# Holding back the loads of piece 12, splitting the transposes of pieces 8 to 11, and ordering the first slices of block 1 bank by bank in a retention-then-FFN kernel

## The chip, the core and the metric

The kernel runs on one core of one Trainium2 chip. The metric is the device time of one execution in microseconds; the time before is the median of three executions. Five engines run side by side, each with its own instruction stream: PE (TensorE, matrix products), DVE (VectorE), ACT (ScalarE), POOL (GpSimd, which here only issues loads) and SP (SyncE, which here issues stores and transposes by DMA). An engine takes its instructions in order; what stands behind a waiting instruction waits too.

## What is computed

Retention (attention with a decaying mask and no softmax) over 8 batches, 8 heads, 576 positions and 64 dimensions, and then a two-layer network with a hard swish over all 4608 tokens:

```python
scores = scale * np.matmul(q, k.transpose(0, 1, 3, 2))
Dmat = np.where(rel >= 0, gamma[:, None, None] ** rel[None, :, :], 0.0)
attn = np.matmul(scores * Dmat[None], v)
x = attn.transpose(0, 2, 1, 3).reshape(B * S, H * D)        # 4608 x 512
h = x @ w_in                                                # 512 -> 2048
out = (h * np.clip(h + 3.0, 0.0, 6.0) / 6.0) @ w_out        # 2048 -> 512
```

## The kernel before

**Pieces.** The retention part is cut into pieces of 128 positions with all heads. Each batch has four "main" pieces (512 positions), and the last 64 positions of two batches together make one "rest" piece. Pieces 0 to 3 are batch 0, 4 to 7 batch 1, 8 to 11 batch 2, 12 the first rest, 13 to 16 batch 3 and so on. A piece needs its K (`kn`), its Q and V (`qv`), both transposed (`qk`), Q and V scaled by powers of the decay (`vs`), masked scores (`at`), and a state carried from piece to piece (`u` is the sum of products on PE, `ts` the scaled state on DVE, `tbd` its fp16 block-diagonal form, two copies on ACT, L394 and L395). The result `o` is copied by ACT into `xt16`, the transposed tokens (L353).

**Blocks.** The network takes 512 tokens at a time (nine blocks). GEMM1 of a block has 16 units: four matmuls into one PSUM bank `ph` (L409), then ACT's `Relu` (L416), then DVE's minimum and product into `gt` (L417), which frees the bank. There are four such banks. GEMM2 has 16 units of four matmuls (`pout`, L467); every fourth unit of a row group ends with ACT's copy (L471) and a store on SP (L453; L457 for the last block, whose rows go to two places and take two stores).

**Order.** The order is written out by hand. While block kb runs through GEMM2, the pieces of block kb+1 are computed between its units: `put(units, steps)` runs a unit, then one entry of a list `later`, then what `steps` names for that unit. `ahead(c)` prepares piece c: it loads up to piece c+4 (`load_until`) and calls `transposes_by_dma(c)`: SP transposes K, DVE scales Q and V (L306), SP transposes the scaled Q (L303). Pieces 0 to 7 are transposed on PE (`transposes_early`, `transposes`), since the first blocks can't wait for the DMA. `warm` multiplies zeros to keep PE busy at the start (L175).

**Loads.** All loads stand in POOL's stream in the order of the pieces, three to a piece (K, Q, V; six half ones for a rest piece, L91), with the weights between pieces 3 and 5 (L97, L102). The loads share eight semaphores in turn, so each one waits until the eighth load before it has landed. There are nine buffers for `kn` and `qv`, so the load of piece c also waits until piece c-9 was used.

**Block 1's first units.** Between GEMM2 of block 0 and the rest of GEMM1 of block 1, the program opens all four banks and calls `g1_columns` three times: columns 0 to 255 of all four banks, then `second_half(7)` (the result and state of piece 7), then columns 256 to 383 of all banks, then `ahead(8)`, then columns 384 to 511 of all banks, which are piece 7's tokens. As the last slice of a bank is done, ACT and DVE take that bank.

Of the kernel before, what the change touches and what calls it, by code (L numbers as in the profile page):

```python
# [13 lines left out]
ALU = mybir.AluOpType  # L14
# [3 lines left out]
def kernel(  # L18
# [66 lines left out]
    def load(c, behind_q=None):  # L85
        kn = nat.tile([P, H, D], FP16, tag="kn", bufs=9, name=f"kn_{c}")
        qv = nat.tile([P, 2, H, D], FP16, tag="qv", bufs=9, name=f"qv_{c}")
        loaded[c] = {"kn": kn, "qv": qv, "q16": qv[:, 0]}
        for dst, src in ((kn, k), (qv[:, 0], q), (qv[:, 1], v)):
            for p0, b, s0, n in pieces[c][3]:  # L90
                nc.gpsimd.dma_start(dst[p0:p0 + n],  # L91
                                    src[b, :, s0:s0 + n, :].rearrange("h s d -> s h d"))
            if src is q and behind_q is not None:
                behind_q()

# [18 lines left out]
    first = const.tile([P, 1], FP32)  # L114
# [17 lines left out]
    for p in range(NPAIR):  # L132
# [17 lines left out]
                            in1=gq[:, :, None].to_broadcast([P, H, P]), op=ALU.mult)  # L150
# [6 lines left out]
    gqv = const.tile([P, 2, H, D], FP16)  # L157
# [3 lines left out]
    tbd = []  # L161
# [8 lines left out]
    def warm(n, cols):  # L170

        w = psum.tile([P, MBLK], FP32, tag="ph", bufs=4, name=f"warm_{warmed[0]}")
        warmed[0] += 1
        for _ in range(n):
            nc.tensor.matmul(w[:, 0:cols], zeros[:, 0:P], zeros[:, 0:cols],  # L175
                             start=True, stop=True)
# [13 lines left out]
    st = {}  # L190
    later = []
# [14 lines left out]
    def transposes_early(c, alone=True):  # L206
        kn, q16 = loaded[c]["kn"], loaded[c]["q16"]
        qk = work.tile([P, 2, NPAIR, P], FP16, tag="qk", bufs=6, name=f"qk_{c}")
        st[c]["qk"] = qk
        pk = psum.tile([P, NPAIR, P], FP16, tag="ph", bufs=4, name=f"trk_{c}")  # L210
        for p in range(NPAIR):
            nc.tensor.transpose(pk[:, p, :], kn[:, 2 * p:2 * p + 2, :], ident16)
        nc.scalar.copy(qk[:, 1], pk)
        if c == 0:
            warm(6, MBLK)
        elif alone:
            warm(8, P)
        pq = psum.tile([P, NPAIR, P], FP32, tag="ph", bufs=4, name=f"trq_{c}")
        for p in range(NPAIR):
            for h2 in range(2):  # L220
                r = slice(h2 * HALF, h2 * HALF + HALF)
                nc.tensor.matmul(pq[r, p, :], q16[:, 2 * p + h2, :], dq[:, 2 * p + h2, :],
                                 start=(p == 0), stop=(p == NPAIR - 1), skip_group_check=True)
        nc.scalar.copy(qk[:, 0], pq)  # L224
        if c == 0:
            warm(8, P)

    def scores_last(c):

# [63 lines left out]
                nc.tensor.transpose(ps[:, i, p, :], src[:, 2 * p:2 * p + 2, :], ident16)  # L293
        nc.vector.tensor_copy(qk, ps)

    def transposes_by_dma(c):
        qv, kn = loaded[c]["qv"], loaded[c]["kn"]
        qk = work.tile([P, 2, NPAIR, P], FP16, tag="qk", bufs=6, name=f"qk_{c}")
        vs = work.tile([P, 2, H, D], FP16, tag="vs", bufs=6, name=f"vs_{c}")
        st[c] = {"qk": qk, "vs": vs[:, 1]}  # L300

        def transpose(which, src):
            nc.sync.dma_start_transpose(qk[:, which], src.rearrange("s h d -> s (h d)"))  # L303

        transpose(1, kn)
        nc.vector.tensor_tensor(out=vs, in0=qv, in1=gqv, op=ALU.mult)  # L306
        transpose(0, vs[:, 0])

    def scores(c):
        run_later(9)  # L310
# [58 lines left out]
                                     stop=(j == len(cs) - 1 and p == NPAIR - 1),  # L369
                                     skip_group_check=True)  # L370

    def update_state(c):
        kind, b, i, _ = pieces[c]
        if kind == "rest":
            return
        u = st[c]["u"]
        scale = gc_b[1 if i == PER - 1 and b % 2 else 0]
        ts = work.tile([P, NPAIR, D], FP16, tag="ts", bufs=2, name=f"ts_{c}")
        if i == 0:
            nc.vector.tensor_tensor(out=ts, in0=u, in1=scale, op=ALU.mult)  # L380
        else:
            ta = work.tile([P, NPAIR, D], FP32, tag="ta", bufs=2, name=f"ta_{c}")
            nc.vector.tensor_tensor(out=ta, in0=u, in1=st[c - 1]["ts"], op=ALU.add)  # L383
            nc.vector.tensor_tensor(out=ts, in0=ta, in1=scale, op=ALU.mult)  # L384
        st[c]["ts"] = ts
        old = state_of.get(b)
        new = free_tbd.pop(0)
        state_of[b] = new
        if old is not None and st[c].get("o") is not None:
            free_tbd.append(old)  # L390
        elif old is not None:
            st[c]["before"] = old
            st[c]["last_reader"] = True
        nc.scalar.copy(tbd[new][0:HALF, :, 0:D], ts[0:HALF])  # L394
        nc.scalar.copy(tbd[new][HALF:P, :, D:2 * D], ts[HALF:P])  # L395

    def finish(c):
        intra(c)
# [13 lines left out]
    def g1_act(kb, ph, fc):  # L412
        if kb not in gts:
            gts[kb] = work.tile([P, NFC, MBLK], FP16, tag="gt16", bufs=2, name=f"gt16_{kb}")
        u = work.tile([P, MBLK], FP32, tag="moeu", bufs=3, name=f"u_{kb}_{fc}")
        nc.scalar.activation(u, ph, ACTF.Relu, bias=cb[:, 0:1], scale=1.0 / 6.0)  # L416
        nc.vector.scalar_tensor_tensor(out=gts[kb][:, fc, :], in0=u, scalar=1.0,  # L417
                                       in1=ph, op0=ALU.min, op1=ALU.mult)
# [6 lines left out]
        g1_mm(kb, ph, fc, range(NCC))  # L425
        g1_act(kb, ph, fc)

    def g1_columns(kb, banks, cols):

        t0 = kb * MBLK  # L430
        for fc, ph in enumerate(banks):
            for dmc in range(NCC):
                nc.tensor.matmul(ph[:, cols], win16[:, dmc, P * fc:P * fc + P],
                                 xt16[:, dmc, t0 + cols.start:t0 + cols.stop],
                                 start=(cols.start == 0 and dmc == 0),
                                 stop=(cols.stop == MBLK and dmc == NCC - 1),
                                 skip_group_check=True)
                if dmc == NCC - 1 and cols.stop == MBLK:
                    g1_act(kb, ph, fc)

    def g1_first(kb):

# [7 lines left out]
    def store(kb, mc, cols, src):  # L450
        if kb < B:
            r0 = kb * S + P * mc
            nc.sync.dma_start(out[r0:r0 + P, cols], src)  # L453
        else:
            for i in range(2):
                r0 = (2 * mc + i) * S + MAIN
                nc.sync.dma_start(out[r0:r0 + HALF, cols], src[i * HALF:i * HALF + HALF])  # L457

    pouts = {}

# [35 lines left out]
    load(4)  # L496
    for i in range(4):
        load_wout(4 * i, 4 * i + 4)
    for c in (5, 6, 7):
# [35 lines left out]
    def second_half(c):  # L535
        inter(c)
        finish(c)

    def ahead(c):
        if c < NP:  # L540
            load_until(c + 4)
            transposes_by_dma(c)

    def scores_second(c):

# [50 lines left out]
    def gemm1(kb, steps):  # L596

        units = {0: [lambda: g1_first(kb)]}.get(kb, [])
        done = {0: 2, 1: 4}.get(kb, 0)
        put(units + [unit1(kb, f) for f in range(done, NFC)], steps)  # L600

    gemm1(0, {12: [(scale, 4)]})
# [1 line left out]
    put([unit2(0, mc, part) for mc, part in order],  # L606
        {0: [(transposes, 4)], 2: [(scores, 4)], 4: [(second_half, 4)],
         8: [(make_mask_rest,)], 10: [(early, 5)], 11: [(scores, 5)], 12: [(early, 6)],
         13: [(second_half, 5), (scores, 6)], 14: [(early, 7)],
         15: [(second_half, 6), (scores, 7)]})  # L610
    run_later(9)

    banks = [g1_bank(1, fc) for fc in range(4)]
    g1_columns(1, banks, slice(0, 2 * P))
    second_half(7)
    g1_columns(1, banks, slice(2 * P, 3 * P))
    ahead(8)
    g1_columns(1, banks, slice(3 * P, MBLK))
    gts.pop(0)


    gemm1(1, {2: [(ahead, 9)], 5: [(ahead, 10)], 8: [(ahead, 11)]})
    AT = {1: (-1, 7), 4: (-1, 7, 12), 5: (-1, 3, 7, 11)}
    for kb in range(1, NMB - 1):
        mine, next_ = of_block(kb + 1), of_block(kb + 2)
        pairs = [mine[i:i + 2] for i in range(0, len(mine), 2)]
        steps = {}
        for j, ended, begun in zip(AT[len(mine)], [[]] + pairs, pairs + [[]]):
            steps.setdefault(j, []).append((step, ended, begun))
        for c in mine[4:]:  # L630
            steps.setdefault(2, []).append((ahead, c))
        for c, j in zip(next_[:4], (12, 13, 14, 15)):
            steps.setdefault(j, []).append((ahead, c))
        put([unit2(kb, mc, part) for mc in range(MBLK // P) for part in range(4)], steps)
        gts.pop(kb)
        gemm1(kb + 1, {})
# [34 lines left out]
```

## Time and profile before

| what | value |
|---|---|
| median of 3 executions | 310.43 us (310.31 to 310.57) |
| the profiled execution | 311.39 us, of which the span 309.6 us |
| PE busy | 299.5 us (97%) |
| DVE, ACT, POOL busy | 185.8, 173.6, 108.0 us |
| loads (q0, POOL's queue) | 18.36 MB, packets 82.9% of 16 engines' span |
| stores and transposes (q1, SP's queue) | 16.79 MB, packets 27.6% |
| one load of 128 KB, issue to landing | median 6.2 to 6.5 us |
| one transpose, issue to landing | median 4.1 us, 2.4 to 8.8 |
| granted TensorE clock | 1.00 in every slice |

The profiled execution is one run with the hardware profiler on; its time is 1.8 us more than its span. In the timelines below a line gives the start, the length, the engine, the line of the kernel, the operation, its operands and sizes, and in brackets the idle time of the engine before it and what ended that. In the list of waits the numbers are microseconds in total, times, and the longest. Stretches in which an engine with slack is idle cost nothing.

### The profile page before, as it was taken

What the parts mean: (1) busy time and instruction counts of PE and PEld (TensorE: products, weight loads), DVE (VectorE), ACT (ScalarE), POOL (GpSimd) and SP (SyncE); (2) the same over time, 40 slices, a digit from 0 to 9 for tenths busy, and PEclk for the clock granted to TensorE, in tenths of its full rate; (3) what the DMA queues carried; (4) which work ended last, traced back from release to release, by engine and by line L of the source; (5) the groups of instructions that cost most, each with busy time, mean ns of one, the idle gap of its engine ahead of it and who ended that gap; (6) DMA issues with size and microseconds to landing.
All of it is one profiled execution on the core that took longest, in us unless ns stands there. A gap on an engine that the chain in (4) does not pass through costs nothing.

```text
span 309.6 us, 5856 instructions
## 1 busy us (share of the span) xinstructions
PE 299.5 (97%) x2286; PEld 152.6 (49%) x2286; DVE 185.8 (60%) x310; ACT 173.6 (56%) x298; POOL 108.0 (35%) x135
## 2 busy tenths in 40 slices
PE   8889999899999999999999999999999999999994
PEld 3644446544544554445544644455445544444443
DVE  4758715796737882885478737856688357207600
ACT  4657356773457554854574737644765467227611
POOL 8974378696735390045353720130000000000000
PEclk9999999999999999999999999999999999999999
DMA  9999999999999999539998996094423230010033
GB/s 65 145 197 190 204 156 211 168 140 156 191 174 170 114 171 163 118 24 154 146 166 74 140 184 138 17 123 69 104 51 53 83 55 0 34 70 34 1 70 68
DMA packets 153164, 35.52 MB, mean 115 GB/s; under 512 B 143792, under 2 KB 148656, under 8 KB 153136
## 3 DMA queue, kind: packets, MB, share of 16 engines
q0 software_dynamic: 117264, 18.36, 82.9%
q1 hardware_dynamic: 35872, 16.79, 27.6%
q8 instruction: 18, 0.29, 0.4%
q14 instruction: 10, 0.08, 0.1%
HBM read 36.70 MB, written 9.44 MB: 149 GB/s over the span
## 4 chain that ended last, share of the span: by engine, by line
PE 76%; DMA 16%; POOL 6%; issue 1%; DVE 0%; ACT 0%; POOLq 0%
PE pout L467 35%; PE ph L409 31%; DMA wout<-in_moe_w_out_dram 5%; POOL qv L91 4%; DMA win<-in_moe_w_in_dram 3%; DMA qv<-in_v_dram 3%; PE o L349 3%; DMA kn<-in_k_dram 3%; DMA qk<-vs 2%; POOL kn L91 2%; PE o L338 2%; PE sc L316 2%; PE u L367 1%; PE pout L480 1%; PE sc L552 1%
## 5 line engine op out<-in xcount | busy, mean ns | idle before, releaser
L417 DVE SCALAR_TENSOR_TENSOR gt<-u,ph 128x512 f16<-128x512 f32 x144 | 98.1, 687 | 69.0 <-ACT u L416 68.3
L467 PE MATMUL pout<-wout,gt 128*128 128x512 f16 x560 | 126.6, 380 | 0.0
L409 PE MATMUL ph<-xt,win 128*128 128x512 f16 x560 | 122.3, 379 | 1.4 <-DVE gt L417 1.4
L416 ACT ACTIVATE u<-ph,cb 128x512 f32<-128x512 f32 x144 | 98.5, 687 | 25.9 <-PE ph L409 25.4
L409 PEld LDWEIGHTS <-win 128*128 128x128 f16 x560 | 54.7, 98 | 67.3 <-issue 1.6
L467 PEld LDWEIGHTS <-gt 128*128 128x128 f16 x560 | 52.3, 98 | 60.8
L91 POOL DMA_DIRECT2D kn<-in_k_dram x40 | 34.4, 861 | 80.9 <-PE u L367 59.2
L471 ACT COPY osb<-pout 128x512 f32<-128x512 f32 x35 | 20.5, 585 | 48.1 <-PE pout L467 47.8
L91 POOL DMA_DIRECT2D qv<-in_q_dram x40 | 34.2, 858 | 7.4 <-DMA wout<-in_moe_w_out_dram 3.0
L320 DVE TENSOR_TENSOR at<-sc,mask_wide 128x1024 f16<-128x1024 f32 x19 | 23.2, 1223 | 22.4 <-PE sc L316 22.4
L91 POOL DMA_DIRECT2D qv<-in_v_dram x40 | 34.6, 868 | 3.2 <-DMA wout<-in_moe_w_out_dram 1.7
L394 ACT COPY tbd<-ts 64x256 f16<-64x256 f16 x28 | 11.3, 405 | 34.1 <-DVE ts L384 17.2
L353 ACT CAST xt<-o 128x512 f16<-128x512 f32 x35 | 19.3, 588 | 10.9 <-PE o L349 10.7
L306 DVE TENSOR_TENSOR vs<-qv,gqv 128x1024 f16<-128x1024 f16 x28 | 17.9, 684 | 0.0
L560 DVE TENSOR_TENSOR at<-sc,mask_wide 128x512 f16<-128x512 f32 x24 | 15.4, 681 | 0.0
L349 PE MATMUL o<-at,vs 128*64 128x128 f16 x280 | 12.2, 223 | 0.0
L395 ACT COPY tbd<-ts 64x256 f16<-64x256 f16 x28 | 11.2, 401 | 0.4
L383 DVE TENSOR_TENSOR ta<-u,ts 128x256 f32<-128x256 f32 x21 | 8.7, 416 | 3.6 <-PE u L367 3.6
L316 PE MATMUL sc<-qk 64*128 64x128 f16 x184 | 9.1, 218 | 1.2 <-ACT qk L224 1.1
L338 PEld LDWEIGHTS <-tbd 128*128 128x128 f16 x124 | 7.9, 98 | 4.5
L384 DVE TENSOR_TENSOR ts<-ta,gc 128x256 f16<-128x256 f32 x21 | 8.9, 425 | 1.7
L349 PEld LDWEIGHTS <-vs 128*64 128x64 f16 x280 | 8.6, 109 | 2.6 <-issue 0.4
(73 smaller groups left out, 120.1 us busy)
## 6 DMA issues: line engine op xcount, KB each, us to landing
out_dram<-osb SPq DMA_DIRECT2D x32, 256.0 KB, 3.5
kn<-in_k_dram POOLq DMA_DIRECT2D x32, 128.0 KB, 6.2
qv<-in_q_dram POOLq DMA_DIRECT2D x32, 128.0 KB, 6.3
qv<-in_v_dram POOLq DMA_DIRECT2D x32, 128.0 KB, 6.5
wout<-in_moe_w_out_dram POOLq DMA_DIRECT2D x4, 512.0 KB, 15.2
win<-in_moe_w_in_dram POOLq DMA_DIRECT2D x3, 512.0 KB, 10.1
out_dram<-osb SPq DMA_DIRECT2D x6, 128.0 KB, 2.3
win<-in_moe_w_in_dram POOLq DMA_DIRECT2D x2, 256.0 KB, 6.2
```

The lines of the kernel that those rows point to most:

```text
L91: nc.gpsimd.dma_start(dst[p0:p0 + n], src[b, :, s0:s0 + n, :].rearrange("h s d -> s h d"))
L306: nc.vector.tensor_tensor(out=vs, in0=qv, in1=gqv, op=ALU.mult)
L316: nc.tensor.matmul(sc[:, h2, p, :], qk[r, 1, p, :], qk[r, 0, p, :], start=True, stop=True)
L320: later.append(lambda: nc.vector.tensor_tensor(out=at.rearrange("t a b s -> t (a b) s"), in0=sc.rearrange("t a b s -> t (a b) s"), in1=mas ...
L349: nc.tensor.matmul(o[r, p, :], vs[:, 2 * p + h2, :], at[:, h2, p, :], start=(st[c]["first"] and p == 0), stop=(p == NPAIR - 1), skip_group ...
L353: nc.scalar.copy(xt16[:, :, g0:g0 + P], o)
L409: nc.tensor.matmul(ph, win16[:, dmc, P * fc:P * fc + P], xt16[:, dmc, t0:t0 + MBLK], start=(dmc == 0), stop=(dmc == NCC - 1))
L416: nc.scalar.activation(u, ph, ACTF.Relu, bias=cb[:, 0:1], scale=1.0 / 6.0)
L417: nc.vector.scalar_tensor_tensor(out=gts[kb][:, fc, :], in0=u, scalar=1.0, in1=ph, op0=ALU.min, op1=ALU.mult)
L467: nc.tensor.matmul(pout, gt[:, fc, P * mc:P * mc + P], wout16[:, fc, :], start=(fc == 0), stop=(fc == NFC - 1))
L471: nc.scalar.copy(osb, pout)
L560: nc.vector.tensor_tensor(out=at[:, h2], in0=banks[h2], in1=mask[:, None, :].to_broadcast([P, NPAIR, P]), op=ALU.mult)
```

## The change

Six edits:

1. `warm(8, P)` becomes `warm(2, MBLK)`: two matmuls of 512 columns for eight of 128, at four places.
2. `transposes_by_dma` is split in `transpose_k` and `transpose_q` (which also scales). K of piece 8 is transposed inside GEMM2 of block 0; Q of 8 ahead of piece 7's result; K and Q of 9 to 11 at units 0, 1, 5 and 9 of block 1's GEMM1. The loads of pieces 8 to 11 are issued from an earlier place in the program; POOL's order stays the same.
3. `ahead_last(11)`: the first load of piece 12 waits for DVE's scaling of piece 11.
4. `g1_columns` takes one bank at a time, and the last two slices go in an order in which bank 0 is complete after three groups of four matmuls. Piece 7's two state copies on ACT are put behind the fifth unit's activation.
5. In the last block the second store of each pair goes to ACT's queue.
6. The fifth piece of a block is prepared after unit 0 in place of unit 2. The instruction order of no engine changes by this.

```diff
@@ load
-                nc.gpsimd.dma_start(dst[p0:p0 + n],
-                                    src[b, :, s0:s0 + n, :].rearrange("h s d -> s h d"))
+                loaded[c]["dma"].append(nc.gpsimd.dma_start(
+                    dst[p0:p0 + n], src[b, :, s0:s0 + n, :].rearrange("h s d -> s h d")))
@@ transposes_early
         elif alone:
-            warm(8, P)
+            warm(2, MBLK)
...
         if c == 0:
-            warm(8, P)
+            warm(2, MBLK)
@@
-    def transposes_by_dma(c):
-        qv, kn = loaded[c]["qv"], loaded[c]["kn"]
+    def transpose_k(c):
         qk = work.tile([P, 2, NPAIR, P], FP16, tag="qk", bufs=6, name=f"qk_{c}")
+        st[c] = {"qk": qk}
+        nc.sync.dma_start_transpose(qk[:, 1], loaded[c]["kn"].rearrange("s h d -> s (h d)"))
+
+    def transpose_q(c):
         vs = work.tile([P, 2, H, D], FP16, tag="vs", bufs=6, name=f"vs_{c}")
-        st[c] = {"qk": qk, "vs": vs[:, 1]}
...
+        st[c]["vs"] = vs[:, 1]
+        scaled = nc.vector.tensor_tensor(out=vs, in0=loaded[c]["qv"], in1=gqv, op=ALU.mult)
+        nc.sync.dma_start_transpose(st[c]["qk"][:, 0], vs[:, 0].rearrange("s h d -> s (h d)"))
+        return scaled
@@ update_state(c, copies_later=False)
-        nc.scalar.copy(tbd[new][0:HALF, :, 0:D], ts[0:HALF])
-        nc.scalar.copy(tbd[new][HALF:P, :, D:2 * D], ts[HALF:P])
+        def copies():
+            nc.scalar.copy(tbd[new][0:HALF, :, 0:D], ts[0:HALF])
+            nc.scalar.copy(tbd[new][HALF:P, :, D:2 * D], ts[HALF:P])
+        if copies_later:
+            later.append(copies)
+        else:
+            copies()
@@ store
-                nc.sync.dma_start(out[r0:r0 + HALF, cols], src[i * HALF:i * HALF + HALF])
+                queue = nc.scalar if i else nc.sync
+                queue.dma_start(out[r0:r0 + HALF, cols], src[i * HALF:i * HALF + HALF])
@@
+    def ahead_last(c):
+        scaled = transpose_q(c)
+        load_until(c + 4)
+        tc.add_manual_dep(
+            loaded[c + 1]["dma"][0].ins, scaled.ins.name,
+            mybir.DependencyInfo(mybir.DependencyClass.Sync, mybir.DependencyReason.DATA),
+            reason="transposes of block 2 first")
@@ the main order
+    load_until(11)
...
-         13: [(second_half, 5), (scores, 6)], 14: [(early, 7)],
+         13: [(second_half, 5), (scores, 6)], 14: [(early, 7), (transpose_k, 8)],
...
-    g1_columns(1, banks, slice(0, 2 * P))
-    second_half(7)
-    g1_columns(1, banks, slice(2 * P, 3 * P))
-    ahead(8)
-    g1_columns(1, banks, slice(3 * P, MBLK))
+    for fc in range(4):
+        g1_columns(1, fc, banks[fc], slice(0, 2 * P))
+    transpose_q(8)
+    inter(7)
+    intra(7)
+    update_mm([7])
+    update_state(7, copies_later=True)
+    third, fourth = slice(2 * P, 3 * P), slice(3 * P, MBLK)
+    for fc, cols in ((0, third), (1, third), (0, fourth), (2, third), (1, fourth), (3, third),
+                     (2, fourth), (3, fourth)):
+        g1_columns(1, fc, banks[fc], cols)
...
-    gemm1(1, {2: [(ahead, 9)], 5: [(ahead, 10)], 8: [(ahead, 11)]})
+    gemm1(1, {0: [(transpose_k, 9)], 1: [(transpose_q, 9), (transpose_k, 10)],
+              5: [(transpose_q, 10), (transpose_k, 11)], 9: [(ahead_last, 11)]})
...
-            steps.setdefault(2, []).append((ahead, c))
+            steps.setdefault(0, []).append((ahead, c))
```

More of the change, by code (lines that the diff above doesn't have):

```diff
@@ L87, in load @@
         qv = nat.tile([P, 2, H, D], FP16, tag="qv", bufs=9, name=f"qv_{c}")
-        loaded[c] = {"kn": kn, "qv": qv, "q16": qv[:, 0]}
+        loaded[c] = {"kn": kn, "qv": qv, "q16": qv[:, 0], "dma": []}
         for dst, src in ((kn, k), (qv[:, 0], q), (qv[:, 1], v)):
             for p0, b, s0, n in pieces[c][3]:
-                nc.gpsimd.dma_start(dst[p0:p0 + n],
-                                    src[b, :, s0:s0 + n, :].rearrange("h s d -> s h d"))
+                loaded[c]["dma"].append(nc.gpsimd.dma_start(
+                    dst[p0:p0 + n], src[b, :, s0:s0 + n, :].rearrange("h s d -> s h d")))
             if src is q and behind_q is not None:
@@ L294, in transposes @@
         nc.vector.tensor_copy(qk, ps)
-    def transposes_by_dma(c):
-        qv, kn = loaded[c]["qv"], loaded[c]["kn"]
+    def transpose_k(c):
         qk = work.tile([P, 2, NPAIR, P], FP16, tag="qk", bufs=6, name=f"qk_{c}")
+        st[c] = {"qk": qk}
+        nc.sync.dma_start_transpose(qk[:, 1], loaded[c]["kn"].rearrange("s h d -> s (h d)"))
+    def transpose_q(c):
         vs = work.tile([P, 2, H, D], FP16, tag="vs", bufs=6, name=f"vs_{c}")
-        st[c] = {"qk": qk, "vs": vs[:, 1]}
[L302 to L307, printed above, removed]
+        st[c]["vs"] = vs[:, 1]
+        scaled = nc.vector.tensor_tensor(out=vs, in0=loaded[c]["qv"], in1=gqv, op=ALU.mult)
+        nc.sync.dma_start_transpose(st[c]["qk"][:, 0], vs[:, 0].rearrange("s h d -> s (h d)"))
+        return scaled
     def scores(c):
@@ L370, in update_mm, with update_state @@
                                      skip_group_check=True)
-    def update_state(c):
+    def update_state(c, copies_later=False):
         kind, b, i, _ = pieces[c]
@@ L426, in g1, with g1_columns @@
         g1_act(kb, ph, fc)
-    def g1_columns(kb, banks, cols):
+    def g1_columns(kb, fc, ph, cols):
         t0 = kb * MBLK
[L431 to L439, printed above, removed]
+        for dmc in range(NCC):
+            nc.tensor.matmul(ph[:, cols], win16[:, dmc, P * fc:P * fc + P],
+                             xt16[:, dmc, t0 + cols.start:t0 + cols.stop],
+                             start=(cols.start == 0 and dmc == 0),
+                             stop=(cols.stop == MBLK and dmc == NCC - 1),
+                             skip_group_check=True)
+        if cols.stop == MBLK:
+            g1_act(kb, ph, fc)
     def g1_first(kb):
@@ L498 @@
         load_wout(4 * i, 4 * i + 4)
-    for c in (5, 6, 7):
+    for c in range(5, 8):
         load(c)
@@ L541, in ahead @@
             load_until(c + 4)
-            transposes_by_dma(c)
+            transpose_k(c)
+            transpose_q(c)
+    def ahead_last(c):
[5 more added lines that the diff above has]
+            reason="transposes of block 2 first")
     def scores_second(c):
```

## The prediction

> **What bounds the kernel now.** The page says PE is busy for 299.5 of 309.6 us, so I looked first for where it is not. Three views were read in this order: the chain that ended last (from 71 us on it is PE without a break until the last ACT copy at 305.34), the list of PE's waits, and the timelines of single engines around those waits. PE's waits, in whole (us in total, times, longest):
>
> ```profile
> PE ph L409 <- DVE gt L417: 1.4, 1, 1.4
> PE warm L175 <- DVE cb L112: 1.3, 1, 1.3
> PE sc L316 <- ACT qk L224: 1.1, 2, 0.8
> PE trq L222 <- DMA qv<-in_q_dram: 0.9, 1, 0.9
> PE sc L552 <- DMA qk<-vs: 0.6, 1, 0.6
> PE o L258 <- DVE at L240: 0.3, 1, 0.3
> ```
>
> So at most these 5.6 us and the tail after 305.3 can be won; any larger change must be a loss. The PE timeline places them (start, length, then the idle time in brackets):
>
> ```profile
> 14.97 0.61 PE L175 MATMUL warm<-zeros 128*128 128x128 f16 x8
> 16.44 0.41 PE L222 MATMUL trq<-dq,qv 128*64 128x128 f16 x8 [0.86 <-DMA qv<-in_q_dram]
> ...
> 56.07 1.96 PE L433 MATMUL ph<-xt,win 128*128 128x128 f16 x32
> 59.47 10.52 PE L409 MATMUL ph<-xt,win 128*128 128x512 f16 x48 [1.44 <-DVE gt L417]
> 69.92 0.40 PE L316 MATMUL sc<-qk 64*128 64x128 f16 x8
> 70.96 0.40 PE L552 MATMUL sc<-qk 64*128 64x128 f16 x8 [0.64 <-DMA qk<-vs]
> ```
>
> The change works on the third (fewer zeros before 19 us), on the 1.44 and on the 0.64, and on the tail.
>
> **Fewer zeros: 0.** Eight matmuls of 128 columns hold PE for 0.54 us (9.69 to 10.23 around piece 1); two of 512 columns hold it for 0.44 (0.219 each, L409: 13.99 us for 64). That is 0.1 us at each of four places, and all four lie before the wait at 16.44. Query load 3 was issued at 10.53 and landed 5.9 us later, at 16.43: PE waits for it whatever it does before. Without that cover it would be worth 0.3 to 0.4 us. On the cost side: the first nine zeros took 4.02 us, 0.446 each, against 0.219 later, so PE does start at half speed, while the granted clock reads 1.00 throughout. [...]
>
> **Bank by bank, copies later, piece 8 scaled first: -0.78.** Now ACT and DVE go like this:
>
> ```profile
> 56.05 0.58 ACT L353 CAST xt<-o 128x512 f16<-128x512 f32 x1 [0.94 <-PE o L349]
> 57.17 0.40 ACT L394 COPY tbd<-ts 64x256 f16<-64x256 f16 x1 [0.53 <-DVE ts L384]
> 57.59 0.40 ACT L395 COPY tbd<-ts 64x256 f16<-64x256 f16 x1
> 58.01 3.21 ACT L416 ACTIVATE u<-ph,cb 128x512 f32<-128x512 f32 x5
> ```
>
> ```profile
> 54.18 1.22 DVE L320 TENSOR_TENSOR at<-sc,mask_wide 128x1024 f16<-128x1024 f32 x1
> 56.18 0.42 DVE L383 TENSOR_TENSOR ta<-u,ts 128x256 f32<-128x256 f32 x1 [0.78 <-PE u L367]
> 56.71 0.43 DVE L384 TENSOR_TENSOR ts<-ta,gc 128x256 f16<-128x256 f32 x1
> 57.05 0.68 DVE L306 TENSOR_TENSOR vs<-qv,gqv 128x1024 f16<-128x1024 f16 x1
> 58.73 3.21 DVE L417 SCALAR_TENSOR_TENSOR gt<-u,ph 128x512 f16<-128x512 f32 x5 [1.00 <-ACT u L416]
> ```
>
> PE's 32 short matmuls are eight groups of four at 0.245 us. Bank 0 ends with the fifth group, at 57.30, but ACT first does two state copies and starts on bank 0 only at 58.01. With the change the last slice of bank 0 is the third group. It needs piece 7's tokens (L353 ends at 56.63), so it runs from 56.68 to 56.93. ACT starts 0.2 us after a bank's end (59.47 + 2 x 0.863 = 61.20, next activation at 61.40): 57.13, with the copies out of the way. DVE follows 0.72 us after ACT (58.01, 58.73), at 57.85, and PE 0.74 us after that (58.73, 59.47): **58.59 instead of 59.47, -0.88**. PE's own groups end at 58.15 (the wait for L353 costs 0.12, inside the remaining idleness of 0.44). Piece 8's scaling, moved ahead of L383 on DVE, fits the gap of 0.78 us: V of piece 8 landed at 52.53 (chain), DVE is free at 55.40 and needs 0.68, to 56.08.
>
> What is late next: the two copies (0.84) now stand on ACT behind the fifth activation, at 60.33, so activations 5 to 7 are late, and piece 9's scaling (now one activation pair earlier on DVE) stands between gt 5 and gt 6. Stepping ACT by 0.64 and DVE by 0.64 back to back, gt 6 starts at 63.13, and PE's seventh 512-column unit, due at 58.59 + 6 x 0.863 = 63.77, would start at 63.87: +0.10. All other units have slack. Bounds of this step: 0 if the queues refill behind each other, -1.32 if no idleness is left.
>
> **K and Q of pieces 8-11 apart, loads of 12 on held back: -0.64.** On PE this touches one wait, for piece 9's Q transpose: issued on SP at 64.30 after its scaling, landed at 70.83, 6.5 us; all eight transposes issued from 53.67 to 69.70 took 6.5 to 8.8. Now the scaling runs after gt 5, 62.5 to 63.2, and the issue is at 63.2. PE is there at 58.69 + 12 x 0.863 + 0.33 = 69.38. So a landing within 6.2 us costs nothing. The nearest rows for a transpose with few loads beside it are those issued between 95 and 125 us (2.4 to 7.4, median 3.3); the last load ahead of it, V of piece 11, lands at 62.1 (issued 53.92, 8.2). I take 4: landing 67.2, the wait of 0.64 goes whole. [...]
>
> K of piece 8 passes the store of block 0's last rows on SP. It waits for its load (issued 42.61, about 8 us), so SP issues it near 50.6 for 1.3 us, and the store is not ready before 53.2 (L471 at 52.61 + 0.58). Behind each Q transpose on SP stands the next K transpose; 11 is issued near 69.6, due at 77.2 on PE.
>
> The added wait stands on POOL. Behind it are all loads from piece 12 on, nothing else:
>
> ```profile
> 54.88 1.40 POOL L91 DMA_DIRECT2D kn<-in_k_dram  x2
> ...
> 61.61 0.88 POOL L91 DMA_DIRECT2D kn<-in_k_dram  x1 [1.08 <-PE ph L409]
> ...
> 79.51 0.88 POOL L91 DMA_DIRECT2D kn<-in_k_dram  x1 [1.33 <-PE sc L316]
> ```
>
> Piece 12 starts at 54.88 now; then it waits for piece 11's scaling, after gt 13, done near 69.55: 14.7 us later. Six halves of 0.68 and nine loads of 0.87 follow; V of piece 15 is issued at 80.6. Loads in the quiet beginning landed 3.6 to 5.9 us after issue, those of 79.5 to 84 us 7.4 to 8.2; between them I take 6: 86.6. DVE scales piece 15 directly ahead of block 2's first gt, which must end at 90.45 so that PE's fifth unit of block 2 (88.47 - 1.42 + 4 x 0.863 = 90.50) does not wait: scaling may start at 89.1. It hides, with 2.5 us to spare. Later loads catch up: POOL idles 59 us in waits for freed buffers (L91 on PE u L367). The piece-16 and later fifth transposes move two steps ahead in the code, but on no engine does the order of instructions change: 0.
>
> **Second half stores on ACT: -0.5.** At the end SP issues two 64 KB stores one after the other:
>
> ```profile
> 302.45 4.38 SPq L457 DMA_DIRECT2D out_dram<-osb  x6
> ```
>
> Ten such issues take 466/562/588 ns (min/median/max); the last starts at 306.2 and lands about 2 us later, which ends the span. With the other half on ACT both start near 305.7. ACT's own issue is in no row: at SP's 0.56 it saves 0.56; at POOL's 0.88, 0.24; at SP's transpose issue of 1.2 nothing. I take 0.5, close to the nearest row, a store on SP. The earlier stores on ACT stand before copies that come 1.16 us or more of idleness later, so delay none.
>
> **Sum.** -0.88 + 0.10 - 0.64 - 0.5 = -1.92. The profiled execution took 311.39 us (span 309.6 and 1.8 around it), so 309.5; it lies 0.96 above the median of 310.43, and on that **308.5**.
>
> **Rivals.** *The transpose stays slow*: SP issues piece 9's Q at 63.2, and at 7.8 us (the row of the first Q transpose) it lands at 71.0, where it lands now; PE's gain at 59 us is eaten by that wait and only the tail is left: 310.43 + 0.04 - 0.5 = 310.0. For it: all eight rows; against: they all had loads beside them. *The held loads come too late* (slower): each load waits for the landing of the eighth before it, so with a landing time L V of 15 is issued at 73.7 + L, if later than 80.6. From L = 7.7 on it lands after 89.1 and PE waits in block 2; from L = 8.7 on that eats the 1.92. L was 10 between 69 and 73 us: issue 83.7, landing 93.7, PE at 95.1 instead of 90.5, net +2.7: 313.1. For it: that row, and 7.5 at 80 us; against: then eight transposes and the loads' own queue were under way, here one transpose. *More than forecast*: no wait left at 59 us and 0.56 at the tail: 310.43 - 1.32 - 0.64 - 0.56 = 307.9.
>
> **Chances.** Forecast (308.0 to 309.4) 0.70; slow transpose 0.14 (0.08 of it still faster, 0.06 about equal); late loads 0.11; more than forecast 0.05. About 0.2% (0.6 us) is what a measurement of this kernel can tell from no change. Faster 0.83, same 0.06, slower 0.11. The range 307.7 to 310.0 leaves out the late loads and little else.
>
> **What would show it.** Right: PE's wait on gt near 58.6 us at 0.4 to 0.5 in place of 1.44, no wait on L552's successor near 69.4, no new PE wait near 90, the loads of piece 12 from about 69.5, the span's end 0.5 us nearer to the last copy. Wrong: a PE wait for gt in block 2 behind piece 15's scaling, a Q transpose of piece 9 over 6.2 us, or ACT's copies showing as waits of PE between 60 and 65 us.

## The result and the profile after

The changed kernel takes **312.82 us** (median of 11 executions, 311.26 to 316.27) against 310.43 for the kernel before (310.02 to 312.27, 11 executions): slower, by a ratio of 1.0074 with an interval of 1.0044 to 1.0103. The forecast was 308.5. The ratio leaves out one execution, that of 316.27, whose granted clock was 0.988.

The profiled execution took 312.04 us, its span 310.0 (before 309.6), the clock 1.00 throughout. PE's waits in the changed kernel, in whole (total us, times, longest):

```profile
PE u L269 <- DVE vs L203: 1.5, 1, 1.5
PE sc L315 <- DMA qk<-vs: 1.4, 1, 1.4
PE warm L175 <- DVE cb L112: 1.3, 1, 1.3
PE sc L315 <- ACT qk L224: 0.4, 2, 0.3
PE ph L415 <- DVE gt L423: 0.4, 1, 0.4
PE trq L222 <- DMA qv<-in_q_dram: 0.4, 1, 0.4
```

PE's timeline of the changed kernel places them (start, length, idle time before in brackets):

```profile
18.88 0.40 PE L269 MATMUL u<-vs,kn 128*128 128x128 f16 x4 [1.46 <-DVE vs L203]
...
59.49 10.52 PE L415 MATMUL ph<-xt,win 128*128 128x512 f16 x48 [0.44 <-DVE gt L423]
69.94 0.40 PE L315 MATMUL sc<-qk 64*128 64x128 f16 x8
70.18 0.39 PE L568 MATMUL sc<-qk 64*128 64x128 f16 x8
...
112.91 0.40 PE L315 MATMUL sc<-qk 64*128 64x128 f16 x8 [1.36 <-DMA qk<-vs]
```

Of the two waits that the change aimed at, 1.44 has become 0.44 and 0.64 is gone: the scores at 69.94 and 70.18 follow each other. Two others stand in their place: 1.46 at the start, for V of piece 3, and **1.36 at 112.91**, where no wait was before. The first has a like in the kernel before, 0.86 at 16.44 for Q of piece 3, which is 0.40 now. The second is for the transposed Q of piece 16, the fifth piece in block 2's GEMM2. Here are SP's issues of that transpose, of the changed kernel and then of the one before:

```profile
106.32 1.20 SPq L305 DMA_TRANSPOSE qk<-vs  x1
```

```profile
107.02 1.19 SPq L303 DMA_TRANSPOSE qk<-vs  x1
```

Issued 0.7 us earlier than before, it lands after 6.5 us in place of 3.3. PE wants it 5.2 us after the issue in both kernels (112.91 - 1.36 - 106.32). At its issue eight loads are under way (issued and not landed) in the changed kernel, two in the kernel before. The DMA view of the stretch from 106 to 112 us shows what moved beside it: first the loads' queue of the changed kernel, then that of the kernel before (packets, MB, packet time as a share of 16 engines' span; the times of packets that overlap add up, so it can pass 100%).

```profile
q0 software_dynamic: 5351, 0.67, 240.2%
```

```profile
q0 software_dynamic: 3714, 0.47, 124.4%
```

POOL's timeline tells where these loads come from. The changed kernel:

```profile
54.90 0.89 POOL L91 DMA_DIRECT2D qv<-in_v_dram  x1
70.86 1.38 POOL L91 DMA_DIRECT2D kn<-in_k_dram  x2 [15.07 <-PE u L366]
...
81.82 1.02 POOL L91 DMA_DIRECT2D qv<-in_v_dram  x1
...
103.14 0.87 POOL L91 DMA_DIRECT2D qv<-in_v_dram  x1 [1.35 <-DMA kn<-in_k_dram]
105.69 0.69 POOL L91 DMA_DIRECT2D kn<-in_k_dram  x1 [1.68 <-DMA qv<-in_q_dram]
```

And the kernel before around the same time:

```profile
87.41 0.88 POOL L91 DMA_DIRECT2D qv<-in_v_dram  x1
94.03 1.36 POOL L91 DMA_DIRECT2D kn<-in_k_dram  x2 [5.74 <-DMA qk<-kn]
...
103.40 0.89 POOL L91 DMA_DIRECT2D kn<-in_k_dram  x1 [5.28 <-PE u L367]
```

The wait of 15.07 us is the hold; the bracket names PE, but DVE's scaling of piece 11 ended at 70.33, half a microsecond before the load starts. Before, POOL pauses at 88 and 98 us for a free buffer, and the DMA engines catch up (the load issued at 87.41 lands after 10.6 us, that at 94.03 after 5.5). After, POOL's idle time at 103 and 105 us ends on landings of earlier loads, each time 0.3 us behind that of the eighth load before: nothing waits for a buffer, the queue itself is behind. Its loads issued from 88.6 to 96 us land after 12 to 16 us; those of 94 to 98 us in the kernel before, after 5.5 to 7. The first load of piece 21 starts at 105.69, at 94.03 before: of the 15 us that the loads were held, 11.7 have not been made up when piece 16 needs a quick transpose.

Milestones that answer to the prediction's steps, from PE's timelines of before and after: start of block 0's GEMM1 to the start of block 1's long GEMM1 run 39.92 and 39.07 (-0.85); from there to the start of GEMM2's first 32 matmuls 12.20 and 11.49 (-0.71); start of the last ACT copy to the end of the span 4.25 and 3.93 (-0.32). The start of GEMM1 is 0.87 later, the new wait costs 1.4. Together that is about +0.4, the difference of the two spans.

The medians differ by 2.39, not by 0.4. The profiled execution of before lies 0.96 above its median, that of the changed kernel 0.78 below its own: 7 of the 11 executions of the changed kernel have a granted clock under 0.996, and the profiled one has not (more on that below). The rest, some 0.3 us, lies outside the span: an execution's time is 1.8 us more than its span in the kernel before and 2.0 to 2.1 in every kernel that holds the loads until piece 11 is scaled (after, and e1, e6, e8, e9, e13 and e14 below). No view shows what that is; it stays open.

### The profile page after: what moved, and what is told of

Same layout as the page of the kernel before. It is cut to its first block, busy times and chain, and to the rows that moved or that the text cites. A ratio compares the mean times of both kernels' runs of the same rounds, so it can differ in the third digit from the quotient of the medians.

```text
span 310.0 us, 5801 instructions
## 1 busy us (share of the span) xinstructions
PE 300.3 (97%) x2262; PEld 151.6 (49%) x2262; DVE 185.6 (60%) x310; ACT 173.3 (56%) x298; POOL 107.9 (35%) x135
## 4 chain that ended last, share of the span: by engine, by line
PE 87%; DMA 4%; POOL 3%; DVE 2%; ACT 1%; issue 1%; POOLq 0%; ACTq 0%
PE ph L415 39%; PE pout L473 37%; PE o L348 3%; DMA qv<-in_v_dram 2%; DMA qk<-vs 2%; POOL qv L91 2%; PE sc L315 2%; PE o L337 2%; POOL kn L91 1%; PE pout L486 1%; PE u L366 1%; PE ph L438 1%; ACT u L422 1%; PE sc L568 1%; DVE gt L423 0%
## 5 line engine op out<-in xcount | busy, mean ns | idle before, releaser
L91 POOL DMA_DIRECT2D qv<-in_q_dram x40 | 34.9, 875 | 7.5 <-DMA wout<-in_moe_w_out_dram 3.6
L175 PE MATMUL warm<-zeros 128*128 128x512 f16 x23 | 8.8, 525 | 1.3 <-DVE cb L112 1.3
```

Source lines behind the costliest of these rows:

```text
L91: loaded[c]["dma"].append(nc.gpsimd.dma_start(dst[p0:p0 + n], src[b, :, s0:s0 + n, :].rearrange("h s d -> s h d")))
```

## The experiments

Sixteen kernels ran in four groups, e1 to e4 and so on; each ratio is to executions of the kernel before on the same chip (medians 310.81, 310.56, 310.98, 310.68 in the four groups). My theory H: the added wait on POOL pushes the loads' backlog to piece 16's transpose. Rival Z: the fewer zeros cost the time, by a late or slow start.

**e1 to e4: one part undone.** e1 puts the old zeros back, e2 takes the added wait out, e3 does both, e4 puts only the fewer zeros into the kernel before.

```diff
e1, e3:  -            warm(2, MBLK)        +            warm(8, P)      (two calls)
e2, e3:  -        tc.add_manual_dep(loaded[c + 1]["dma"][0].ins, scaled.ins.name, ...)
e4, in the kernel before:  -  warm(8, P)   +  warm(2, MBLK)             (two calls)
```

> The changed kernel with the eight short zero matmuls put back at all four places, everything else as changed. Theory Z (fewer zeros let the granted PE clock fall in some executions, and that is what spreads the times from 311.3 to 316.3 us): all executions at a clock of 1.00, a spread under 0.8 us, and a median lower by 0.5 to 1.5 us, near 311. Theory H (the loads held back are the whole loss, through the 1.4 us that PE waits near 112 us for piece 16's Q transpose): no change against the changed kernel, 312 to 313 us, clocks as often below 1.00 as there. In both the wait near 112 us stays, as the loads are still held.

> The changed kernel without the wait of piece 12's first load on piece 11's scaling; everything else as changed, the few zeros too. Theory H: the wait for piece 16's Q transpose near 112 us goes (1.4 us), Q of piece 9 still lands in time or nearly, and the median falls by 1 to 1.5 us, to some 311.4. Theory Z: the spread and the clocks below 1.00 stay, and the median stays over 310.4.

> Both put back: old zeros, no held loads; what is left of the change is the bank order, the later copies, the early transposes and the stores on ACT. Theories Z and H together: 308.3 to 309.0 us with a narrow spread, faster than before by 1.4 to 2.1 us. Z alone: near 310; H alone: near 311 with a wide spread. If neither is the cause, it stays at 312 to 313.

> The kernel before with two zero matmuls of 512 columns in place of eight of 128, nothing else changed. Theory Z: the median rises over 311 us, executions differ by 2 us and more, and several show a granted clock under 1.00. Theory H: 310.4 us, as before, with the old narrow spread.

Measured: e1 311.57 us, 1.0031 [1.0013, 1.0050]; e2 309.43, **0.9962** [0.9944, 0.9979]; e3 309.35, 0.9963 [0.9948, 0.9978]; e4 311.25, 1.0028 [1.0005, 1.0050]. Without the added wait the change is a gain. PE's timeline of e2 at the same place has no bracket:

```profile
111.07 0.61 PE L337 MATMUL o<-qk,tbd 128*128 128x128 f16 x8
111.61 0.40 PE L315 MATMUL sc<-qk 64*128 64x128 f16 x8
```

The transpose lands after 4.6 us in e2 and 4.4 in e3. In e1 the wait is 1.73. H holds; Z alone doesn't, as e1 stays slower than before. Nor was the hold needed for piece 9: in e3 the Q transposes issued between 53 and 72 us take 4.7 to 8.0 us (after: 2.4 to 8.4, median 3.0), and PE still waits for none of them at 69 us. The hold was not without use: in two of the later profiles without it (e11 and e16) PE waits 0.27 and 0.59 us near 78 us for Q of piece 11, and in none with the full hold.

**e5 to e8: one part alone, and the dose.** e5 puts the second stores on ACT in the kernel before; e6 adds the hold alone to the kernel before; e7 holds the loads only until piece 9 is scaled (old zeros); e8 keeps the whole hold, with the old zeros, and prepares the fifth piece earlier, after unit 9 of the GEMM1 ahead.

```diff
e5  +  queue = nc.scalar if i else nc.sync
    +  queue.dma_start(out[r0:r0 + HALF, cols], src[i * HALF:i * HALF + HALF])
e6  +  load_until(15); tc.add_manual_dep(loaded[12]["dma"][0].ins, scaled.ins.name, ...)   (piece 11)
e7  -  5: [..., (transpose_k, 11)], 9: [(ahead_last, 11)]
    +  1: [(transpose_q_then_load, 9), ...], ... 9: [(transpose_q, 11)]
e8  -  for c in mine[4:]: steps.setdefault(0, []).append((ahead, c))
    -  gemm1(kb + 1, {})
    +  gemm1(kb + 1, {9: [(ahead, c) for c in next_[4:]]})
```

> The kernel before with the second store of each pair of the last block on ACT's queue, nothing else changed. By the profiles of the changed kernel the time from the last ACT copy's start to the end of the span is 3.9 us with ACT's queue and 4.3 to 4.8 without, so 0.3 to 0.8 us faster than before (forecast in the prediction: 0.5). If the store on ACT gives nothing, the same as before.

> The kernel before with the held loads alone (the first load of piece 12 waits for the scaling of piece 11); zeros, bank order, transposes and stores as before. Theory H: piece 16's Q transpose again takes over 6 us and PE waits 1 to 2 us for it near 113 us, in part of the executions followed by some 3.4 us at half the granted clock (1.7 us more); the wait of 0.64 us near 71 us may go. Net 0.5 to 2.5 us slower than before. Rival (the held loads only hurt together with the rest of the change, since PE reaches that place 0.7 us sooner there): no wait near 113 us and no loss.

> The changed kernel with the old zeros, and the loads of piece 12 held only until piece 9 is scaled (about 62.5 us in place of 69.6). Theory H, graded: the loads are 7 us late instead of 15, so the backlog is gone by 106 us; piece 16's Q transpose lands in under 5 us, no wait of PE near 111 us, 308.6 to 309.6 us, as without any hold. Rival: any hold costs; the wait stays at about 1 us or more.

> The changed kernel with the old zeros and the full hold, but the fifth piece of a block (16, 25 and so on) scaled and transposed within GEMM1 of the block before (after its tenth unit) and not in GEMM2. If the loss is that one late transpose, it is then issued near 99 us, lands by 107 and PE does not wait near 111 us: 308.6 to 309.6 us with the hold still in. Rival: the held loads cost elsewhere too (other transposes, contention): over 310.4 us.

Measured: e5 310.37, 0.9987 [0.9971, 1.0003], too near 1 to decide on time alone; its profile shows 3.93 us from the last copy to the end, 4.25 before. e6 311.30, **1.0039** [1.0010, 1.0068]: the hold alone makes the old kernel slower. PE's timeline of e6:

```profile
113.53 0.61 PE L317 MATMUL sc<-qk 64*128 64x128 f16 x8 [2.42 <-DMA qk<-vs]
```

The transpose lands after 7.5 us there, and the eight matmuls behind the wait last 0.61 us, not 0.40 as in the rows above (more on that below). e7 309.55, 0.9972 [0.9955, 0.9989]: under half of the hold (POOL idles 6.8 us in it, 15.1 in after), landing 4.8, no wait. e8 309.48, **0.9956** [0.9940, 0.9971], with the hold still in. SP's timeline of e8:

```profile
99.23 2.36 SPq L305 DMA_TRANSPOSE qk<-vs  x1
```

This one lands after 8.3 us, the slowest of all for piece 16's Q, and PE does not wait, as it is issued 7 us earlier. So it is the lateness of this one issue under the backlog that costs, and not the backlog elsewhere, but for the 0.3 us outside the span, which e8 has too.

**e9 to e12: the zeros, and a version that combines.** e9 is e8 with the fewer zeros; e10 is the kernel before without any zeros at the four places; e11 is e8 without the hold; e12 repeats e4.

```diff
e9   -  warm(8, P)    +  warm(2, MBLK)          (in e8, two calls)
e10  -  elif alone: warm(8, P)     -  if c == 0: warm(8, P)     (in the kernel before)
e11  -  tc.add_manual_dep(...)                  (in e8)
```

> The kernel of e8 (full hold, fifth piece prepared within GEMM1) with the few zeros of the change. If fewer zeros cost nothing: the ratio of e8, 0.994 to 0.997. If fewer zeros delay the start (in three profiles with few zeros V of piece 3 was scaled at 17.4, 18.4 and 18.5 us, in seven with the old zeros at 16.4 to 17.6): 0.5 to 1 us more, 0.996 to 0.999, and V of piece 3 again after 17.5 us.

> The kernel before without any zero matmuls at the four places that the change touches (the first nine and the six after K of piece 0 stay). If the zeros there matter through the granted clock, PE's matmuls before 20 us take their half-speed length (0.4 us for 512 columns) more often and the kernel is slower by 1 us or more. If PE is bound there by the loads of piece 3 alone: within 0.5 us of before.

> The kernel of e8 without the hold (old zeros, bank order, early transposes, stores on ACT, fifth piece prepared within GEMM1). If the hold is of no use to Q of piece 9: the same as e8 and e3, 309.0 to 309.7 us, no wait of PE near 69 and near 111 us. If the hold helps: 0.3 us or more slower than e8.

> The kernel of e4 once more (before with few zeros), since its interval of 1.0005 to 1.0050 hardly leaves 1 out. If fewer zeros cost: again 1.001 or more and V of piece 3 scaled after 17.3 us; if not: the interval takes in 1 and that scaling falls near 16.7.

Measured: e9 309.89, 0.9971 [0.9949, 0.9993]; e10 311.81, 1.0026 [1.0002, 1.0049]; e11 309.19, **0.9935** [0.9911, 0.9959], the lowest ratio here, though on six executions and with an interval that overlaps those of e8, e2 and e3; e12 310.66, 0.9994 [0.9975, 1.0014], which doesn't repeat e4's 1.0028. e10 fits neither of its expectations cleanly: some 0.8 us slower in the median, with a full clock in its profile and 5 of 12 executions under 0.996.

**e13 to e16: the four corners on one chip.** The changed kernel (e13), with the old zeros (e14), without the hold (e15), with neither (e16); the edits are those of e1 to e3.

> The changed kernel once more, side by side with its three neighbours. Its four undisturbed executions (clock 1.0) lay 1.6 us above before's median, those of the same kernel with the old zeros only 0.6 above, on another chip. Theory A (fewer zeros cost nothing while the clock stays full, and the 1 us belonged to the chip or the execution): executions at a clock of 0.996 or more lie within 0.4 us of those of the run with the old zeros beside it. Theory B (fewer zeros cost about 1 us beside the wait): they lie 0.8 to 1.2 us above. On the clock, both: if short idleness near piece 16 and a thinner start each bring drops, over a third of the executions are below 0.996 (7 of 11 before); if the drops were that chip's, fewer than 2 of 12.

> The changed kernel with the zeros of before: some 0.3% above before (1.0031 the first time), 2 to 4 of 12 executions at a clock below 0.996, and piece 16's Q transpose landing 6 us or more after its issue, PE waiting 1.3 to 2.4 us for it. Theory A: equal to the run before it within 0.4 us at a full clock; theory B: 0.8 to 1.2 us faster.

> The changed kernel without the added POOL wait, fewer zeros: 0.4% below before (0.9962 the first time), no wait for piece 16. Theory A: within 0.4 us of the run with the old zeros behind it. Theory B, if the zeros cost 1 us in any company: 0.8 to 1.2 us above it; if only in company of the wait: equal. Clock below 0.996 in 0 to 3 of 12.

> Neither the added POOL wait nor fewer zeros: 0.4% below before (0.9963 the first time); no execution below a clock of 0.996, as in all 50 so far of kernels with the old zeros and no wait for piece 16.

Measured: e13 313.28, 1.0082 [1.0064, 1.0101]; e14 311.77, 1.0053 [1.0030, 1.0076]; e15 309.69, 0.9973 [0.9952, 0.9993]; e16 309.89, 0.9977 [0.9964, 0.9989]. With the hold the fewer zeros cost: among executions at a clock of 0.996 or more, the medians are 312.33 (three executions only) and 311.56, 0.8 apart (1.06 in the first pair, after allowing for the chips: +1.62 and +0.56 over before). Without it they cost nothing (309.67 and 309.89; e2 and e3, 309.43 and 309.36). Nor do they show a cost in e9, which has the hold but not the late transpose (1.39 under before at a full clock; e8, with the old zeros, 1.08). That is theory B in its second form, "only in company of the wait", on few executions; what joins two edits that lie 40 us apart is not shown.

The profile of e16 also corrects H: with no hold at all, the transpose took 6.2 us once, and PE waited 1.1 us. So the hold doesn't create this risk but makes it the rule (one profile of each kernel):

| kernels | landing of piece 16's Q, us | PE's wait, us |
|---|---|---|
| old order, no hold (before, e4, e5, e10, e12) | 3.3, 4.2, 4.3, 4.7, 4.5 | 0 |
| changed order, no hold (e2, e3, e15, e16) | 4.6, 4.4, 5.1, 6.2 | 0, 0, 0, 1.1 |
| hold until piece 9 (e7) | 4.8 | 0 |
| hold until piece 11 (after, e1, e6, e13, e14) | 6.5, 6.8, 7.5, 7.6, 7.5 | 1.4, 1.7, 2.4, 2.5, 2.4 |

**The clock behind the waits.** e13's profiled execution has a mean granted clock of 0.989 and a span of 314.6. PE's timeline of e13 around its two long waits:

```profile
19.01 0.40 PE L269 MATMUL u<-vs,kn 128*128 128x128 f16 x4 [2.05 <-DVE vs L203]
...
115.90 0.40 PE L315 MATMUL sc<-qk 64*128 64x128 f16 x8 [2.53 <-DMA qk<-vs]
...
117.44 4.69 PE L473 MATMUL pout<-wout,gt 128*128 128x512 f16 x16
```

and its stretches of 2 us (length, busy time of PE, PEld, DVE, ACT, POOL with counts, granted clock, DMA share, GB/s):

```profile
18.00:20.00 2.00, 0.99 (x13) 0.74 (x14) 1.47 (x3) 0.00 (x0) 1.15 (x2) 1.00 1.31 199
20.00:22.00 2.00, 1.84 (x12) 0.78 (x8) 0.15 (x1) 0.75 (x2) 1.22 (x2) 0.66 1.24 206
22.00:24.00 2.00, 2.00 (x6) 0.76 (x5) 0.04 (x1) 0.69 (x1) 0.33 (x1) 0.50 1.24 205
24.00:26.00 2.00, 2.00 (x11) 0.89 (x10) 1.83 (x3) 1.49 (x3) 0.41 (x1) 0.99 1.30 205
...
114.00:116.00 2.00, 0.10 (x4) 0.13 (x6) 0.00 (x0) 0.00 (x0) 0.53 (x2) 1.00 1.50 210
116.00:118.00 2.00, 2.00 (x34) 1.55 (x32) 1.64 (x2) 1.07 (x2) 1.59 (x3) 0.55 2.19 188
118.00:120.00 2.00, 2.00 (x7) 0.69 (x5) 1.92 (x4) 0.81 (x2) 2.00 (x3) 0.59 2.10 191
```

Behind each wait the clock is at a half for 3.4 us (2 x 0.34 / 0.5 + 2 + 0.04 at the start, 1.8 + 1.64 at the other), which costs PE 1.7 us. This wait is thus paid nearly twice, in the executions where it happens. It doesn't always happen, and not by the length of the wait. PE's timelines of e1, of e14 and of e2:

```profile
111.62 0.40 PE L315 MATMUL sc<-qk 64*128 64x128 f16 x8 [1.73 <-DMA qk<-vs]
...
112.64 5.31 PE L473 MATMUL pout<-wout,gt 128*128 128x512 f16 x16
```

```profile
112.41 0.40 PE L315 MATMUL sc<-qk 64*128 64x128 f16 x8 [2.38 <-DMA qk<-vs]
...
113.43 3.63 PE L473 MATMUL pout<-wout,gt 128*128 128x512 f16 x16
```

```profile
19.01 0.40 PE L269 MATMUL u<-vs,kn 128*128 128x128 f16 x4 [2.05 <-DVE vs L203]
```

The wait of 1.73 us slows the matmuls behind it, that of 2.38 us doesn't, and of two waits of 2.05 us at the same place the one in e13 does and the one in e2 doesn't. The clock record in the traces tells them apart. In them the granted clock changes only at edges 3.41 us apart: the stretches at full clock last 13.65, 92.16, 105.81, 109.23, 194.56, 300.37 or 303.79 us, which is 4, 27, 31, 32, 57, 88 and 89 times 3.413, and each of the four drops in mid-kernel (two in e13, one each in e1 and e6) lasts one step. Where the edges lie differs from execution to execution. Counted back from the last drop, behind the end of PE's work, the part of a wait that falls between two edges is:

| wait of PE | its parts between two edges, us | the clock at the next edge |
|---|---|---|
| e13 at 115.90, e6 at 113.53 | 2.53; 2.25 and 0.17 | half |
| e13 at 19.01, e1 at 111.62 | 0.27 and 1.78; 1.73 | half |
| e14 at 112.41 | 1.80 and 0.58 | full |
| before at 59.47, after at 112.91, after at 18.88 | 1.44; 1.36; 0.12 and 1.34 | full |
| e2 at 19.01 | 0.89 and 1.16 | full |

So in these rows a step at half clock followed parts of 2.53, 2.25, 1.78 and 1.73 us, none followed parts of 1.44 us and less, and at 1.7 to 1.8 us both are seen (e14's 1.80 passed free). Waits of 2.38 us (e14) and 2.05 us (e2) that an edge cut in two passed free.

Counting all executions whose mean clock is under 0.996 (one such stretch makes 0.9945; in e3, 0.997, and e4, 0.996, the value comes from the end, where the clock falls at 305.4 and 307.6 us, behind PE's last matmul, and not before):

| kernels | executions under 0.996 |
|---|---|
| old zeros, without the full hold or (e8) without the late transpose: before (beside these runs), e3, e5, e7, e8, e11, e16 | 0 of 187 |
| fewer zeros, no such wait: e2, e4, e9, e12, e15 | 7 of 60 |
| no zeros at the four places: e10 | 5 of 12 |
| the wait, old zeros: e1, e6, e14 | 9 of 34 |
| the wait and fewer zeros: after, e13 | 11 of 18 |

So drops of the clock come with both edits, and with both together most of all. For the hold the traces show how; for the fewer zeros only e13 shows it, in the wait of 2.05 us near 19 us, and no other execution with them that lost clock was profiled.

## Why the prediction was wrong

**The step that failed** is the cost of the added POOL wait, put at nothing: "It hides, with 2.5 us to spare. Later loads catch up: POOL idles 59 us in waits for freed buffers". The first sentence held, barely. V of piece 15 was issued at 81.82 (80.6 forecast, and block 0 began 0.87 later) and landed at 88.7, after 6.9 us rather than 6, so that its scaling began at 88.79, 0.3 us before the 89.1 that the prediction allowed; PE did not wait in block 2's first units. The second sentence was the mistake. It counted idle time over the whole span: of those 59 us only 5.3 lie before 106 us (the wait that ends at 103.40), and 5.7 more behind a K transpose, 11 us for a hold of 15. And it asked when the *held loads* are due, but not who else uses the DMA engines while they catch up. The same prediction priced transposes among loads at 6.5 to 8.8 us and used that for piece 9, yet left the next tight transpose, piece 16's, at the price it has in a quiet stretch. Its row was there: 3.3 us landing, 5.2 us to spare on PE's side. At the prediction's own 7.8 us for a transpose beside loads, it would have given a wait of 2.6 us; 1.4 to 2.5 were measured. With it went a second cost that the prediction left out, the half clock of 3.4 us behind such a wait, 1.7 us in part of the executions.

The rival "held loads come too late" had the right mechanism (a backlog behind the hold) and the wrong place and price: it looked for a wait for gt in block 2 from landings of 7.7 us on. That its 313.1 us lies near the measured 312.82 is chance.

Step by step:

- *What bounds the kernel*: right but for 0.3 us. All else that changed shows in PE's waits, the tail and the clock.
- *Fewer zeros, 0*: half right. The saving of 0.1 us at each place isn't there; PE's timeline of the changed kernel around piece 1 shows it held for 0.52 us, against the 0.54 (9.69 to 10.23) of before:

```profile
9.69 0.59 PE L175 MATMUL warm<-zeros 128*128 128x512 f16 x2
10.21 0.41 PE L222 MATMUL trq<-dq,qv 128*64 128x128 f16 x8
```

The wait of 0.86 us at 16.44 that was to cover it was one execution's: of ten profiles with the old zeros only two others have it (e6 0.53, e7 1.43). Alone the edit is worth 1.0028 and 0.9994 in two runs, and nothing without the hold (e15 against e16). But 7 of 60 executions lose clock, and beside the late transpose it costs 0.8 to 1.1 us more. Three of seven profiles with the fewer zeros (after, e2, e13) show a wait of 1.5 to 2.1 us for V of piece 3 near 19 us, none of those with the old zeros one over 0.5 us; GEMM1 starts at 18.8 to 20.6 us (median 19.4) in the seven, at 18.7 to 20.1 (median 18.9) in the ten. Whether the zeros cause it stays open, since those loads are not issued by PE. That the fewer zeros cost nothing through the clock was the author's estimate, which no run shows: load waits such as the 2.05 us near 19 us, behind which the clock was at a half for 3.4 us in e13 and full in e2, were not in it.
- *Bank by bank, -0.88 + 0.10*: right. -0.85 (39.07 to 39.09 in after, e1, e2, e3, e7, e8 and e14, against 39.91 to 39.95 in the six profiles of the old order), and the remaining wait is 0.44 as forecast. In e9, e11, e15 and e16 the stretch lasts 39.2 to 39.5, with short waits in block 0's GEMM1 (in e15 and e16 0.24 and 0.25 us for the weights), and in e13 40.76, with the clock at a half in it. ACT's timeline of the changed kernel shows the two state copies behind five activations, as priced:

```profile
58.03 3.21 ACT L422 ACTIVATE u<-ph,cb 128x512 f32<-128x512 f32 x5 [0.53 <-PE ph L438]
61.14 0.39 ACT L395 COPY tbd<-ts 64x256 f16<-64x256 f16 x1
61.54 0.40 ACT L396 COPY tbd<-ts 64x256 f16<-64x256 f16 x1
```

PE has no wait between 60 and 65 us, so the 0.10 isn't there.
- *K and Q apart, -0.64*: the wait did go, though the figure was the highest of five. The profiles of e4, e5, e10 and e12, all in the old order without the hold, have 0.48, 0.44, 0.57 and 0.48 (e5's list puts it down to DVE, but Q of piece 9 lands there at 69.93 and the wait ends at 70.06, 0.13 behind, as in the others). And it goes without the hold too: Q of piece 9 lands after 4.7 to 5.6 us in the five profiles of the new order without it (e2, e3, e11, e15, e16) and after 6.3 to 6.5 in the five of the old; which of the edits shortens it was not tested. The transposes between 53 and 72 us fell from medians of 7.6 and 7.7 us (K, Q) to 2.4 and 3.0, by more than half; piece 9's Q, for which the prediction took 4 us, landed after 2.4 (issued at 64.00).
- *Second stores on ACT, -0.5*: right in kind, two thirds of the size. The tail is 0.3 shorter than in the profile of before (3.93 against 4.25; it is 3.92 to 3.94 in every profile with these stores but e7's, 4.21), and ACT's issue, 0.50 us and once 0.76, takes about what SP's does (0.47 to 0.59 in the kernel before, 0.47 to 0.78 in the changed one), as the end of ACT's timeline shows:

```profile
304.72 0.76 ACTq L463 DMA_DIRECT2D out_dram<-osb  x1
306.07 0.37 ACT L490 COPY osb<-pout 128x256 f32<-128x256 f32 x1 [1.38 <-PE pout L486]
306.47 0.50 ACTq L463 DMA_DIRECT2D out_dram<-osb  x1
```

- *Sum*: -1.92 forecast. Without the failed step, e3, e16, e8 and e11 give 0.9963, 0.9977, 0.9956 and 0.9935 of some 310.7, or -1.15, -0.7, -1.4 and -2.0 us. From there to +2.39, in medians against before: with the hold and the old zeros +0.6 and +0.9 at a full clock (e1, e14), with the fewer zeros +1.6 (after, e13), and with the drops of the clock, which a median execution has, +2.4 and +2.6 (after, e13).

What stays open: why fewer zeros cost more beside the late transpose, what delays V of piece 3 in some executions, and what the 0.3 us outside the span are.

## What to carry to other kernels

Here the hold moved the queue's load and didn't remove it (of 15 us, 11.7 were not made up 35 us later): follow such a backlog until it is worked off, and reprice at the busy rate every transfer on the way whose issue has little time to spare (here 5.2 us, against 3.3 us quiet and up to 7.6 us busy). Count idle time as slack only where it lies before the place that needs it. Where such a transfer is found, issuing it earlier can take the place of clearing the way for it: e8 got a gain with the hold in, and e11 without it. Price a wait on PE with the clock that may follow it (here 1.7 us in part of the executions, behind waits of 1.7 to 2.5 us).

## What the runs showed of the hardware that was not expected

- In these traces the granted clock changes only at edges 3.41 us apart (stretches of 13.65 to 303.79 us at full clock), whose place differs by execution. Idleness of PE of 1.73 to 2.53 us between two edges was followed by one step at 0.50 in e1, e6 and e13, 1.44 us and less was not, and a wait of 2.38 us that an edge cut into 1.80 and 0.58 was not (e14). With that step falling on them, 16 matmuls of 512 columns take 4.69 us (e13) and 5.31 us (e1), 3.63 us undisturbed (e14).
- The four transposes issued from 64.0 to 68.3 us in the changed kernel, with at most one load under way, land after 2.4 to 2.5 us; the ten issued from 84.8 to 106.3 us, with seven or eight under way, after 6.5 to 8.5.
- A half store of the last block issued on ACT holds it for 0.50 us (0.76 once) in the changed kernel; on SP it takes 0.47 to 0.59 in the kernel before and 0.47 to 0.78 in the changed one.
